# Issue steps of a prefetch and of two head copies in an attention and channel-mix kernel

## The chip, the cores and the metric

The kernel runs on one core of one Trainium2 chip. The metric is the device time of one execution in microseconds. The core has five engines that run side by side and wait for one another by semaphores: TensorE (PE, with its weight loads listed as PEld), VectorE (DVE), ScalarE (ACT), GpSimd (POOL) and SyncE (SP). SP computes nothing here; it issues DMA transfers, one after the other, in the order in which the program lists them.

## The reference, cut to what matters

Two layers follow each other. The first is attention through 32 inducing points, the second a channel mix with a gate.

```python
B, N, m, C = (4, 12608, 32, 128)      # d_ff = 1024
def mab(q, kv):
    s = scale * (q @ kv.transpose(0, 2, 1))
    s = s - s.max(-1, keepdims=True)
    a = np.exp(s)
    a /= a.sum(-1, keepdims=True) + 1e-09
    return a @ kv
h = mab(I, x)                         # 32 rows that sum up all tokens of a batch
x = mab(x, h)                         # each token attends to these 32 rows
...
xk = mu_k * x + (1.0 - mu_k) * x_prev # x_prev: the token before
xr = mu_r * x + (1.0 - mu_r) * x_prev
k = np.maximum(xk @ w_k, 0.0)
v = k * k @ w_v
r = 1.0 / (1.0 + np.exp(-(xr @ w_r)))
return (r * v).astype(np.float32)
```

## The kernel before

**Tiles and stages.** A batch of 12608 tokens is cut into 24 groups of 512 tokens and one of 320. Four groups make a block of 2048 tokens; a batch has six blocks and the tail. The kernel never forms the output of the first layer. It keeps the attention weights of the tokens towards the 32 rows (R, one tile for each group) and folds the 32 rows into the weights of the channel mix (W). The channel mix then reads R and W.

**The main loop.** It runs over 400 units, one to a step: four batches of 25 groups of 4 units, each unit a quarter of the 1024 hidden columns for one group. Step n does, in this order:

- `up` (L803): PE multiplies R with W into a PSUM tile ps_a of 2 x 512 columns (L809 and L811, four matmuls). There are two ps_a tiles.
- what was put down with `soon(n, ...)`; in the second step of a group then `zgate` (L790, PE at L798 and L799, ACT at L801).
- `square` (L815): VectorE makes k_t, the positive part, from ps_a (L821). Then kh, its square in a shorter format, comes from ACT (L826), or, for the steps in the set `high_vector`, from VectorE (L823). ACT squares k_t in place (L827), and GpSimd forms kl, the rest that kh leaves (L829).
- `store` of a finished pair of groups (VectorE L856, then four DMAs at L864).
- `down` (L832) for the unit of four steps earlier: PE multiplies kh and kl with the second weights (L840, six matmuls).
- what was put down with `at(n, ...)`.

So the order on every engine is written by hand: `at` puts work at the end of a step, `soon` puts it between `up` and the squares.

**The first layer beside it.** While batch b is in the main loop, the first layer of batch b+1 is worked off in blocks of 12 steps (`stage_a`, L326 to L483, first step t of a block). One load from HBM brings a block into xb, 1 MB (`load_x`, L193). There are three xb tiles. `btr(c)` (L339), in steps t-1, t, t+1 and t+3, turns a quarter of it on VectorE (L344) and spreads it with four DMAs of SP into xt (L347). In step t+9 PE makes the scores from xt (L372), VectorE takes their maximum (L375), and the rest of the softmax follows until step t+20. The second attention, for batch b itself, is `stage_b` (L598): its last part, `spread`, moves R into place in steps t+11 to t+14 with DMAs of SP (L593 and L670), which are steps t-1 to t+2 of the next block. All of these DMAs, and the output stores, stand in the one queue of SP.

The load of the next block is put down at the end of `stage_a` (L477 to L483), behind `btr(2)` of the same step:

```python
        for bn, jn in order_a[k + 1:]:
            if jn < NBLK - 1:
                at(t + 1, lambda: load_x(bn, jn))
```

With the second last block of a batch comes a small load of the tail (xl, L186).

**The head.** Before the first step, `head` works off the first layer of batch 0, and `start` (L995 to L1034) lays out the first groups of R. Groups 0 and 1 are made before step 0. Groups 2 and 3 are made in the first steps: ACT and VectorE make their parts in steps 3 and 4 (`high`, `low`), and `put` (L768) turns them with four transposes on PE (L771) into a PSUM tile and copies it to R on ACT (L773). `put` of group 2 is in step 6, that of group 3 in step 8. Group 2 is first read by `up` in step 8, group 3 in step 12.

```python
        for k, (high, low, put) in enumerate(pl1):
            at(3, high)
            at(4, low)
            at(2 * k + 6, put)
```

`high_vector` begins as `{3}` and receives two steps of each block of 12.

Of the kernel before, what the change touches and what calls it, by code (L numbers as in the profile page):

```python
# [19 lines left out]
def kernel(  # L20
# [138 lines left out]
    def groups(j):  # L159

        w = G if j < NBLK - 1 else TAIL // Q
        return [(j * BLK + i * w, w) for i in range(Q)]
# [16 lines left out]
    def load_x(b, j, pair=None, pieces=1):  # L179

        S = batches[b]
        gr = groups(j)
        w = gr[0][1]
        if w < G:
            t = xn_pool.tile([P, Q, C], F32, name="xl", bufs=1)
            nc.sync.dma_start(out=t[:w], in_=x[b, gr[0][0]:, :].rearrange("(i p) c -> p i c", p=w))  # L186
            for i in range(Q):
                S.xn[j, i] = t[:, i:i + 1, :]
            return
        src = x[b, j * BLK:(j + 1) * BLK, :].rearrange("(p s) c -> p s c", p=P)  # L190
        if b > 0:
            t = xn_pool.tile([P, Q * Q, C], F32, name="xb", bufs=3)
            nc.sync.dma_start(out=t, in_=src)  # L193
            S.xb[j] = t
            return
        if pair is not None:
            S.xh[j] = [next(pair).rearrange("p u (k c) -> p (u k) c", c=C) for _ in range(2)]
        else:
            t = xn_pool.tile([P, Q * Q, C], F32, name="xb", bufs=3)
            S.xh[j] = [t[:, :2 * Q, :], t[:, 2 * Q:, :]]  # L200
        n = 2 * Q // pieces
        for h in range(2):
            for o in range(0, 2 * Q, n):
                nc.sync.dma_start(out=S.xh[j][h][:, o:o + n, :], in_=src[:, 2 * Q * h + o:2 * Q * h + o + n, :])
# [121 lines left out]
    def stage_a(b, j, at, t):  # L326
# [8 lines left out]
        jt = NBLK - 1  # L335
# [141 lines left out]
        k = order_a.index((b, j))  # L477
        for bn, jn in order_a[k + 1:]:
            if jn < NBLK - 1:
                at(t + 1, lambda: load_x(bn, jn))  # L480
                if jn == NBLK - 2:
                    at(t + 1, lambda: load_x(bn, jt))
                break  # L483


# [102 lines left out]
    def halo(S, g, far=True):  # L588

        if g == 0:  # L590
            nc.vector.memset(S.R[g].bitcast(F32)[:, 0:1], 0.0)
        elif far:
            nc.sync.dma_start(out=S.R[g].bitcast(F32)[:, 0:1], in_=S.R[g - 1].bitcast(F32)[:, G:G + 1])  # L593
        else:
            nc.vector.tensor_copy(out=S.R[g][:, 0:1], in_=S.R[g - 1].bitcast(F32)[:, G:G + 1])
# [272 lines left out]
    def run(th):  # L868
        for f in th:
            f()  # L870
# [118 lines left out]
    def at(n, f):  # L989
        events.setdefault(n, []).append(f)  # L990

    def soon(n, f):
        early.setdefault(n, []).append(f)

    def start():  # L995

        part0, pl0 = stage_b_head([0, 1])
        part1, pl1 = stage_b_head([2, 3])
        sc0, tu0, df0, ex0, nm0 = part0([0])
        sc1, tu1, df1, ex1, nm1 = part0([1])  # L1000
        sc2, tu2, df2, ex2, nm2 = part1([0, 1])
        (hi0, lo0, put0), (hi1, lo1, put1) = pl0
        box = {}

        def bank():
            return pv.tile([P, G], F32, name="ps_v")

        def gate_bank(s):
            if s == 0:
                box["g"] = bank()  # L1010
            return box["g"][:, s * C:(s + 1) * C]

        wa = [wpart(s, 0, bank) for s in range(2)]
        wb = [wpart(s, 1, bank) for s in range(2)]
        wg = [wpart(s, None, lambda s=s: gate_bank(s)) for s in range(2)]
        assert F // G == 2
        S = batches[0]
        run([gates, sc0, sc1, tu0, df0, ex0, wa[0][0], wa[1][0], tu1, nm0, wa[0][1], hi0, wa[1][1], lo0, wa[0][2], put0,
             df1, ex1, wa[1][2], nm1, hi1, lambda: halo(S, 1, far=False)])
        for n, f in ((0, wb[0][0]), (0, wb[0][1]), (1, wb[1][0]), (1, wb[1][1]), (1, put1)):  # L1020
            soon(n, f)
        for n, f in ((0, lo1), (0, wb[0][2]), (1, wb[1][2]), (1, sc2), (2, tu2), (2, df2), (2, ex2), (3, nm2)):
            at(n, f)
        for prod, high, low in wg:
            at(1, prod)
        for prod, high, low in wg:
            at(1, high)
            at(2, low)
        for k, (high, low, put) in enumerate(pl1):
            at(3, high)  # L1030
            at(4, low)
            at(2 * k + 6, put)
            at(4 * k + 4, lambda k=k: halo(S, k + 2, far=False))
        soon(4, lambda: units[0][0].zgate(first=True))  # L1034

    SEG = 12
    high_vector = {3}
    for b in range(B):
        t = b * UB + (4 if b == 0 else 0)
        for j in range(NBLK - 1):  # L1040
            s = t + SEG * j
            high_vector |= {s + 4, s + 8}
            if b + 1 < B:
                stage_a(b + 1, j, at, s)
            first = b == 0 and j == 0
            stage_b(b, j + 1, at, s + 1 + first, first)
        if b + 1 < B:
            s = t + SEG * (NBLK - 1)
            combine(b + 1, at, s)
            stage_b(b + 1, 0, at, s + 13, b == 0)  # L1050
# [6 lines left out]
    with tc.manual_schedule():  # L1057
        head()
        start()
        for n in range(len(units) + LAG + 2):  # L1060
            grp, u = units[n] if n < len(units) else (None, n % NU)
            old, ou = units[n - LAG] if LAG <= n < len(units) + LAG else (None, 0)
            m = n - LAG - 1
            if 0 <= m < len(units) and units[m][1] == NU - 1:
                units[m][0].gate()
            if grp is not None:
                grp.up(u)
                run(early.pop(n, []))
                if n >= NU and u == 1:
                    grp.zgate()  # L1070
                low = grp.square(u, n in high_vector)
                low(nc.vector if n == end else nc.gpsimd, 0, grp.w)
            if 1 <= m <= len(units) and units[m - 1][1] == NU - 1:
                units[m - 1][0].store()
            if old is not None:
                old.down(ou)
            run(events.pop(n, []))
# [30 lines left out]
```

## Time and profile before

| what | value |
|---|---|
| time, median of 3 runs | 1131.95 us (1128.4 to 1132.33) |
| the profiled execution | 1130.93 us |
| its span, first to last instruction | 1128.7 us |
| granted TensorE clock, mean | 0.996 |
| squares kh on ACT and on VectorE | 351 and 49 |
| loads of x in the main loop's form (L193) | 18 |

The profiled execution is one run of its own; its time is longer than its span by what lies around the first and the last instruction. All rows below are of this one execution, and their times count from the start of its span.

A row of a timeline gives the start, the duration, the engine (SPq is the queue of SP), the line, the operation, out<-in, and, in brackets, how long the engine was idle before it and what ended that. Rows of one tile that follow each other are merged (x4). A row of waits gives who waited for whom, the total in us, how often, and the longest. A row of stretches gives the stretch, its length, the busy time of PE, PEld, DVE, ACT and POOL with the number of instructions, the granted clock, and the share and rate of DMA. Matmuls are pipelined, so a busy PE is not PE at its peak: a step of ten matmuls takes about 2.32 us, though each matmul is listed with 0.4.

### The profile page before, as it was taken

Reading aid. Unit: us, or ns where it says so; the run is one execution under the profiler, and the core shown is the slowest. Engines: PE = TensorE matmul, PEld = TensorE weight load, DVE = VectorE, ACT = ScalarE, POOL = GpSimd, SP = SyncE. Lnnn points to the kernel's source line nnn. Section 1 sums busy time; section 2 is a strip of 40 time slices with the busy share of each in tenths; the row PEclk is TensorE's granted clock in tenths of the full one; section 3 lists DMA queues with packets and bytes.
Section 4 is the critical chain, followed back from the end, with each engine's and each line's share of the span. In section 5 each row is a group of like instructions: output and inputs, shape, how many; then the busy total and the mean of one; then the engine's idle time right before and its main releaser. Section 6 shows DMA issues by size and latency. Waiting matters only on the chain.

```text
span 1128.7 us, 17615 instructions
## 1 busy us (share of the span) xinstructions
PE 1098.4 (97%) x5699; PEld 834.1 (74%) x5699; DVE 912.0 (81%) x1318; ACT 969.8 (86%) x1096; POOL 952.9 (84%) x417
## 2 busy tenths in 40 slices
PE   7889999999999999999999999999999999999997
PEld 5567777777776777777777777777778777777886
DVE  6798889887787999887777889898777888887665
ACT  6588888888888888887998889888889999989996
POOL 2279888888897888898888988888888899999997
PEclk9999999999999999999999999999999999999999
DMA  9024555642334655554144554654223233242212
GB/s 344 4 77 89 112 126 119 139 122 36 60 75 109 133 124 117 118 103 104 23 81 88 111 123 113 134 133 82 50 52 62 44 63 61 56 76 57 44 29 34
DMA packets 264458, 102.30 MB, mean 91 GB/s; under 512 B 234256, under 2 KB 237488, under 8 KB 262064
## 3 DMA queue, kind: packets, MB, share of 16 engines
q1 hardware_dynamic: 263360, 101.10, 41.0%
q8 instruction: 45, 0.74, 0.3%
q14 instruction: 45, 0.37, 0.1%
q10 hardware_dynamic: 1008, 0.10, 0.1%
HBM read 28.07 MB, written 25.82 MB: 48 GB/s over the span
## 4 chain that ended last, share of the span: by engine, by line
PE 78%; DVE 9%; ACT 5%; DMA 3%; issue 3%; SPq 1%; POOL 1%; DVEq 0%; ACTq 0%; POOLq 0%
PE ps_v L840 39%; PE ps_a L809 15%; PE ps_a L811 14%; DVE k_t L821 3%; PE pb_a L372 2%; PE pb_b L616 2%; ACT kh L826 2%; PE ps_v L798 2%; PE ps_v L799 2%; DMA xt<-xs 2%; PE pb_a L441 1%; ACT k_t L827 1%; SPq L347 1%; DMA xb<-in_x_dram 1%; POOL kl L829 1%
## 5 line engine op out<-in xcount | busy, mean ns | idle before, releaser
L829 POOL TENSOR_TENSOR kl<-k_t,kh 128x1024 fp32r<-128x1024 f32 (+1 forms) x399 | 938.5, 2385 | 140.7 <-ACT k_t L827 106.7
L821 DVE TENSOR_SCALAR k_t<-ps_a 128x1024 f32<-128x1024 f32 (+1 forms) x400 | 479.6, 1199 | 146.8 <-PE ps_a L811 123.2
L827 ACT ACTIVATE k_t<-k_t 128x1024 f32<-128x1024 f32 (+1 forms) x400 | 418.4, 1048 | 37.6 <-DVE kh L823 25.6
L826 ACT ACTIVATE kh<-k_t 128x1024 fp32r<-128x1024 f32 (+1 forms) x351 | 364.8, 1039 | 85.2 <-PE ps_v L840 49.5
L809 PE MATMUL ps_a<-R,W 128*128 128x512 f32 (+1 forms) x800 | 324.6, 406 | 4.1 <-ACT R L773 2.8
L811 PE MATMUL ps_a<-R,W 128*128 128x512 f32 (+1 forms) x800 | 314.6, 393 | 0.2 <-DVE W L543 0.2
L840 PE MATMUL ps_v<-kh,wvh 128*128 128x512 f32 (+1 forms) x800 | 247.8, 391 | 0.0
L840 PE MATMUL ps_v<-kl,wvh 128*128 128x512 f32 (+1 forms) x800 | 246.7, 390 | 0.7
L840 PE MATMUL ps_v<-kh,wvl 128*128 128x512 f32 (+1 forms) x800 | 247.0, 390 | 0.0
L809 PEld LDWEIGHTS ps_a<-R,W 128*128 128x128 f32 x800 | 151.2, 189 | 78.0 <-issue 14.4
L840 PEld LDWEIGHTS ps_v<-kl,wvh 128*128 128x128 f32 x800 | 148.5, 188 | 37.6 <-POOL kl L829 5.3
L840 PEld LDWEIGHTS ps_v<-kh,wvh 128*128 128x128 f32 x800 | 149.5, 188 | 34.7
L840 PEld LDWEIGHTS ps_v<-kh,wvl 128*128 128x128 f32 x800 | 149.5, 188 | 33.8
L811 PEld LDWEIGHTS ps_a<-R,W 128*128 128x128 f32 x800 | 150.9, 189 | 31.4 <-DVE W L543 0.8
L845 DVE TENSOR_TENSOR oT<-ps_v,rT 128x512 f32<-128x512 f32 (+1 forms) x100 | 66.6, 666 | 1.8
L856 DVE STREAM_TRANSPOSE ot<-oT 128x512 f32<-128x512 f32 x96 | 67.1, 699 | 0.0
L823 DVE SCALAR_TENSOR_TENSOR kh<-ps_a,k_t 128x1024 fp32r<-128x1024 f32 x49 | 60.0, 1224 | 5.1
L801 ACT ACTIVATE rT<-ps_v 128x512 f32<-128x512 f32 (+1 forms) x99 | 57.8, 584 | 0.3
L344 DVE STREAM_TRANSPOSE xs<-xb 128x512 f32<-128x512 f32 x72 | 49.9, 693 | 0.2
L801 ACT ACT_TABLE_LOAD x31 | 39.8, 1283 | 0.6
L798 PE MATMUL ps_v<-R,W 128*128 128x512 f32 (+1 forms) x99 | 39.0, 394 | 0.4 <-DVE oT L845 0.4
L799 PE MATMUL ps_v<-R,W 128*128 128x512 f32 (+1 forms) x99 | 38.7, 391 | 0.0
(211 smaller groups left out, 618.2 us busy)
## 6 DMA issues: line engine op xcount, KB each, us to landing
out_dram<-ot SPq DMA_DIRECT2D x184, 128.0 KB, 3.3
xb<-in_x_dram SPq DMA_DIRECT2D x18, 1024.0 KB, 6.1
xt<-xs SPq DMA_DIRECT2D x288, 64.0 KB, 2.0
R<-ah SPq DMA_DIRECT2D x184, 64.0 KB, 2.0
R<-al SPq DMA_DIRECT2D x184, 64.0 KB, 2.0
kl<-in_x_dram SPq DMA_DIRECT2D x4, 512.0 KB, 9.5
xb<-in_x_dram SPq DMA_DIRECT2D x4, 512.0 KB, 10.8
W<-ah SPq DMA_DIRECT2D x24, 64.0 KB, 2.0
```

What stands on the lines that cost most here:

```text
L798: nc.tensor.matmul(out=ps[:, :w], lhsT=S.W[0][:, F:WF], rhs=R[:, 1:w + 1], start=True, stop=False)
L799: nc.tensor.matmul(out=ps[:, :w], lhsT=S.W[1][:, F:WF], rhs=R[:, 0:w], start=False, stop=True)
L801: nc.scalar.activation(out=self.rT, in_=ps[:, :w], func=AF.Sigmoid)
L809: nc.tensor.matmul(out=ps[:, c, :w], lhsT=S.W[0][:, cs], rhs=R[:, 1:w + 1], start=True, stop=False)
L811: nc.tensor.matmul(out=ps[:, c, :w], lhsT=S.W[1][:, cs], rhs=R[:, 0:w], start=False, stop=True)
L821: nc.vector.tensor_scalar(out=k, in0=self.ps[:, :, :w], scalar1=0.0, scalar2=None, op0=ALU.max)
L826: nc.scalar.activation(out=kh, in_=k, func=AF.Square)
L827: nc.scalar.activation(out=k, in_=k, func=AF.Square)
L829: return lambda eng, a, z: eng.tensor_tensor(out=kl[:, :, a:z], in0=k[:, :, a:z], in1=kh.bitcast(F32)[:, :, a:z], op=ALU.subtract)
L840: nc.tensor.matmul(out=self.v, lhsT=wt[:, fc, :], rhs=kk[:, c, :], start=(fc == 0 and n == 0), stop=(fc == FC - 1 and n == 2))
L845: nc.vector.tensor_tensor(out=self.oT, in0=self.v, in1=self.rT, op=ALU.mult)
L856: nc.vector.transpose(out=ot[:, o:o + w], in_=self.oT)
```

## The change

Two places in the code, three effects. The load of the next block, and the tail's load, are put down four steps later. `put` of groups 2 and 3 stays in its step but goes from the end of the step to the place between `up` and the squares. The set `high_vector` begins empty instead of with step 3.

```diff
@@ stage_a
             if jn < NBLK - 1:
-                at(t + 1, lambda: load_x(bn, jn))
+                at(t + 5, lambda: load_x(bn, jn))
                 if jn == NBLK - 2:
-                    at(t + 1, lambda: load_x(bn, jt))
+                    at(t + 5, lambda: load_x(bn, jt))
                 break
@@ start
             at(3, high)
             at(4, low)
-            at(2 * k + 6, put)
+            soon(2 * k + 6, put)
             at(4 * k + 4, lambda k=k: halo(S, k + 2, far=False))
@@
-    high_vector = {3}
+    high_vector = set()
```

## The prediction

> **What bounds the kernel now.** I read the page's busy shares and its chain first.
>
> ```profile
> PE 1098.4 (97%) x5699; PEld 834.1 (74%) x5699; DVE 912.0 (81%) x1318; ACT 969.8 (86%) x1096; POOL 952.9 (84%) x417
> ```
>
> ```profile
> PE 78%; DVE 9%; ACT 5%; DMA 3%; issue 3%; SPq 1%; POOL 1%; DVEq 0%; ACTq 0%; POOLq 0%
> ```
>
> ```profile
> xb<-in_x_dram SPq DMA_DIRECT2D x18, 1024.0 KB, 6.1
> xt<-xs SPq DMA_DIRECT2D x288, 64.0 KB, 2.0
> ```
>
> TensorE (PE) is the engine to beat: it is busy 97% of the span and makes up 78% of the chain that ended last. No edit here removes matmuls, so the change can only win back time in which PE waits or runs slowly, and can only lose time by making PE wait elsewhere. DMA is 3% of the chain although it computes nothing: somewhere PE waits for data. The last two rows give the two transfers that matter: the 1 MB load of x into xb takes 6.1 us from issue to landing, a 64 KB piece of xt takes 2.0.
>
> Next I looked for the place. PE consumes xt in the score matmuls of L372, once in a block of 12 steps. I took the stretches from the first L809 matmul of such a step to the first of the next one; the columns are the stretch, its length, then busy times, granted clock and DMA. There are 18 such steps. The first row is an undisturbed one, and seven more are like it; the other ten are longer:
>
> ```profile
> 416.86:420.74 3.88, 3.88 (x22) 2.23 (x20) 3.45 (x5) 3.30 (x5) 3.88 (x2) 1.00 0.81 119
> 151.48:155.87 4.39, 4.39 (x22) 2.36 (x20) 3.63 (x5) 3.55 (x5) 4.39 (x3) 1.00 0.37 81
> 217.50:222.95 5.45, 4.74 (x21) 2.63 (x19) 3.48 (x5) 4.72 (x7) 5.45 (x3) 1.00 0.68 147
> 345.10:353.62 8.52, 5.81 (x21) 2.67 (x20) 4.36 (x5) 7.88 (x9) 8.45 (x4) 0.87 0.73 181
> 383.08:388.00 4.92, 4.92 (x22) 2.62 (x20) 3.29 (x5) 4.29 (x6) 4.92 (x3) 1.00 0.50 107
> 449.67:455.53 5.86, 4.86 (x21) 2.61 (x20) 3.35 (x5) 4.32 (x6) 5.86 (x3) 1.00 0.76 188
> 516.94:522.80 5.86, 4.81 (x22) 2.61 (x20) 3.35 (x5) 3.49 (x6) 5.69 (x3) 1.00 0.69 167
> 621.14:626.87 5.73, 4.85 (x21) 2.54 (x19) 4.39 (x5) 5.67 (x7) 5.63 (x3) 1.00 0.77 197
> 655.77:660.69 4.92, 4.33 (x22) 2.61 (x20) 3.30 (x5) 3.93 (x5) 4.92 (x3) 1.00 0.46 93
> 722.49:728.03 5.54, 4.75 (x22) 2.61 (x20) 3.43 (x5) 4.70 (x6) 5.54 (x3) 1.00 0.63 142
> 789.39:794.38 4.99, 4.99 (x21) 2.49 (x20) 3.36 (x5) 3.60 (x6) 4.99 (x3) 1.00 0.45 96
> ```
>
> Over 3.88 us each they lose, in this order, 0.51, 1.57, 4.64, 1.04, 1.98, 1.98, 1.85, 1.04, 1.66 and 1.11: 17.4 us, with the same matmuls in every one. That is the pool that the first edit fishes in.
>
> Why they are late is seen in the timeline of the SP queue, start and duration first. First come rows of the block behind the 449.67 row, then of the one behind the 345.10 row, the score matmuls of PE there, and a row of SP's waits (total, times, longest):
>
> ```profile
> 443.76 2.42 SPq L347 DMA_DIRECT2D xt<-xs  x4
> 446.27 0.53 SPq L193 DMA_DIRECT2D xb<-in_x_dram  x1
> 446.91 0.52 SPq L593 DMA_DIRECT2D R<-R  x1
> ```
>
> ```profile
> 450.07 2.96 SPq L347 DMA_DIRECT2D xt<-xs  x4
> ```
>
> ```profile
> 344.12 0.58 SPq L193 DMA_DIRECT2D xb<-in_x_dram  x1
> 344.79 2.41 SPq L347 DMA_DIRECT2D xt<-xs  x4
> ```
>
> ```profile
> 351.06 2.63 PE L372 MATMUL pb_a<-xt,indT 128*32 128x512 f32 x8 [2.69 <-DMA xb<-in_x_dram]
> ```
>
> ```profile
> SPq L347 <- DMA xb<-in_x_dram: 11.3, 13, 1.2
> ```
>
> SP issues in order and is behind: the last four xt pieces of the block leave at 450.07, in the very step that consumes them. The load stands ahead of them three times over. It takes an issue slot of 0.64 us (446.27 to 446.91). SP then waits for the load's landing before a later piece (11.3 us in 13 waits, 0.87 each). And pieces issued right behind it queue behind its 1 MB: those of 344.79 leave until 346.6 (three slots of 0.6 later) and would land by 348.6 with 2.0, yet PE starts at 351.06, when the load has landed.
>
> **The load, moved from step 1 to step 5.** At step 5 it stands behind the pieces of step 3. Nothing is added or removed: 18 loads stay 18, and the tail's xl load goes along. It is moved past the R pieces and the xt pieces of SP from 446.91 to 453, in some blocks past an output store as well, and past nothing on another queue. For an ordinary late block the last piece is issued 0.64 earlier (the slot) and its group takes 2.42 instead of 2.96, together 1.18: I take 1.2 off each of 1.98, 1.98 and 1.66, which is 3.6, and the full 0.51, 1.04, 1.04 from those that lose less than 1.2. The 217.50 block has the xl load out of the way too, a second slot of about 0.6, so I take its full 1.57. The 345.10 and 621.14 blocks have the pieces right behind the load; with 2.0 to land they are there before PE asks: 4.64 and 1.85. The 789.39 block has no load to move (it is the last of 18) and keeps its 1.11. Behind the long wait the clock is halved:
>
> ```profile
> 351.34:354.75 3.41, 3.41 (x11) 1.48 (x10) 0.69 (x1) 1.70 (x2) 3.41 (x3) 0.50 0.19 32
> ```
>
> Of these 3.41 us 1.13 lie behind 353.62, in the next step: half of that, 0.56, is lost there and comes back if the halving goes. Sum: 3.6 + 2.59 + 1.57 + 4.64 + 1.85 + 0.56 = 14.8 us.
>
> That the halving goes with the wait is my reading of one place. [...]
>
> What is late next? The load itself. It must land before VectorE copies from xb at the next block's step -1. Three kinds of block:
>
> ```profile
> 460.92 0.71 DVE L344 STREAM_TRANSPOSE xs<-xb 128x512 f32<-128x512 f32 x1
> ```
>
> ```profile
> 411.95 3.25 SPq L347 DMA_DIRECT2D xt<-xs  x4
> 415.43 2.94 SPq L864 DMA_DIRECT2D out_dram<-ot  x4
> ```
>
> ```profile
> 426.48 0.71 DVE L344 STREAM_TRANSPOSE xs<-xb 128x512 f32<-128x512 f32 x1
> ```
>
> ```profile
> 347.30 3.67 SPq L864 DMA_DIRECT2D out_dram<-aT  x4
> ```
>
> ```profile
> 359.63 0.71 DVE L344 STREAM_TRANSPOSE xs<-xb 128x512 f32<-128x512 f32 x1
> ```
>
> ```profile
> DMA to landing us min/median/max: 5.5/6.2/11.8
> ```
>
> Store behind the load: pieces end at 450.07 - 0.64 + 2.42 = 451.9, the load lands 6.1 later at 458.0, VectorE asks at 460.92 - 1.2 = 459.7: 1.7 us to spare. Store ahead of it (step 5 itself): pieces end at 413.7, the store takes 2.94, the load lands at 422.8, VectorE asks at 426.48: 3.7 to spare. First block of a batch, with the aT store ahead: pieces end at 346.5, the store takes 2.4 to 3.67 (four slots of 0.6, or as now), the load lands at 355.1 to 356.3, VectorE asks at 359.63 - 5.2 = 354.4: 0.7 to 1.9 short, at two places. VectorE is ahead of PE (below), so I bound this between 0 and 2 x 1.9 and take **0.5**. What queues behind the load are the output store and the next block's R pieces, which PE reads a block later: nothing. SP's total work is unchanged.
>
> **The copies of groups 2 and 3, and the square of step 3.** The set that sends squares to VectorE loses its 3, so the square kh of unit 3 goes to ScalarE (ACT). This square does move, from one engine to another.
>
> ```profile
> 60.42 1.22 DVE L823 SCALAR_TENSOR_TENSOR kh<-ps_a,k_t 128x1024 fp32r<-128x1024 f32 x1
> ```
>
> ```profile
> 61.67 1.06 ACT L827 ACTIVATE k_t<-k_t 128x1024 f32<-128x1024 f32 x1 [1.86 <-DVE kh L823]
> ```
>
> ```profile
> 61.79 0.47 PE L809 MATMUL ps_a<-R,W 128*128 128x512 f32 x1 [0.66 <-DVE kh L823]
> ```
>
> ```profile
> 72.58 0.57 ACT L773 CAST R<-pb_a 128x512 fp32r<-128x512 f32 x1
> ```
>
> ```profile
> 73.21 0.49 PE L809 MATMUL ps_a<-R,W 128*128 128x512 f32 x1 [2.09 <-ACT R L773]
> ```
>
> ACT is idle for 1.86 us before 61.67, waiting for that very kh. It can make it itself from 60.42 on: with two squares of 1.06 it is done with both at 62.5 to 62.6, where it is done at 62.73 now, and VectorE is 1.22 us ahead. PE's 0.66 at 61.79 goes, since no square on VectorE reads ps_a any more. R's copy of group 2 stands at 72.58 behind the two squares of its step; in front of them it ends 2 x 1.06 = 2.1 us earlier, and PE's wait of 2.09 in front of step 8 goes. New waits: the four transposes that feed the copy now need their PSUM bank from ACT's gate of the step before, at about the time when PE comes to them (bounds 0 and 1.06, one pass of ACT as above; I take 0, because ACT loses its 1.86 of idling just before). The squares behind the copies come 0.57 later and are used four steps on. Sum: 0.66 + 2.09 = **2.7 us**.
>
> Total: 14.8 + 2.7 - 0.5 = 17.0. The profiled execution took 1130.93 (span 1128.7 and 2.2 around it), giving 1113.9; it lies 1.0 below the median of the runs, so against 1131.95 I forecast **1115**.
>
> **Rivals.** *The load comes too late and VectorE stops (slower).* Of 18 loads, three are for a first block and one falls where SP is still idle; fourteen have a near deadline. Two rows on the cushions:
>
> ```profile
> DVE k_t L821 <- PE ps_a L811: 123.2, 141, 2.4
> PEld ps_v L840 <- POOL kl L829: 5.3, 14, 0.6
> ```
>
> VectorE waits for PE 141 times, 0.87 us each: that much delay costs nothing. With margins of 1.7 to 3.7 (middle 2.7) the turning point is a landing of 6.1 + 2.7 + 0.9 = 9.7 us. At the longest landing seen, 11.8, it costs 14 x 2.1 = 29 us: 1115 + 29 = **1144**. For it: the load now shares the queues with an output store. Against it: of the loads inside the loop the median is 6.1. [...] Chance 0.07.
>
> *SP is late by itself.* The 789.39 step loses 1.11 without any load ahead. If backlog rather than the load is the cause in the ordinary late blocks, only the two blocks whose pieces stand right behind a load gain: 4.64 + 1.85 + 0.56 + 2.7 = 9.8, **1122**. The same figure comes if the start gives nothing and half of the ordinary blocks stay late. Chance 0.21.
>
> *Another wait takes the place.* POOL's kl ends PE's waits 14 times already (5.3 us), at 84% busy. If PE, once ahead, meets kl or ACT's squares in the steps behind, the gain is given back: about **1130**. Against it: POOL's idle time is 16% of the span. Chance 0.11.
>
> **How the numbers follow.** Forecast (1110 to 1118.5): 0.59; better than 1110, by something outside the sum: 0.02; rivals 0.21, 0.11, 0.07. The range 1110 to 1126 leaves out 0.20. A difference of 0.5% (5.7 us) is about what a measurement can tell: faster 0.82, same 0.11, slower 0.07.
>
> **What would show it.** Right: the ten steps at 3.88 but for three near 4.6 and the last at 5.0; no halved clock behind 350; no PE wait for R near 73; the load's issue behind the xt pieces; 48 squares on VectorE. Wrong: L344 waiting for xb by more than 1 us, PE waiting for kl in the steps behind the scores, or the xt pieces no earlier.

## The result, and the profile after

| | before | after |
|---|---|---|
| time, median (lowest to highest) | 1131.49 us (1127.04 to 1132.41, 6 runs) | 1118.66 us (1115.97 to 1120.37, 6 runs) |
| the profiled execution (its span) | 1130.93 us (1128.7) | 1118.96 us (1116.7) |
| squares kh on ACT and on VectorE | 351 and 49 | 352 and 48 |

The ratio is 0.9895, with a 95% interval from 0.9873 to 0.9917. The change makes the kernel about 1% faster: 12.8 us by the medians and 12.0 by the profiled executions, where 17.0 were forecast. The time lies inside the range of 1110 to 1126, but as near to the 1122 of the rival *SP is late by itself* as to the forecast of 1115; the time alone doesn't choose between them.

First the page of the changed kernel: the busy shares, the chain, the group of VectorE's copies out of xb, and the load of x.

```profile
PE 1094.6 (98%) x5699; PEld 831.1 (74%) x5699; DVE 910.9 (82%) x1317; ACT 969.8 (87%) x1097; POOL 952.8 (85%) x417
...
PE 85%; DVE 7%; ACT 3%; issue 2%; DMA 1%; POOL 1%; SPq 1%; DVEq 0%; POOLq 0%; ACTq 0%
...
L344 DVE STREAM_TRANSPOSE xs<-xb 128x512 f32<-128x512 f32 x72 | 49.9, 694 | 4.3 <-DMA xb<-in_x_dram 3.8
...
xb<-in_x_dram SPq DMA_DIRECT2D x18, 1024.0 KB, 5.7
```

DMA falls from 3% of the chain to 1%, and PE's share grows from 78% to 85%. The third row is new: VectorE has to wait 3.8 us for the load.

Next the steps with scores, in the view of stretches that the prediction used (stretch, length, busy times of PE, PEld, DVE, ACT and POOL, clock, DMA). Two rows are other steps: 346.59 is the one behind the score step of 342.01, and 485.20 is an early step of the next block.

```profile
150.23:154.37 4.14, 4.14 (x22) 2.36 (x20) 3.35 (x5) 3.84 (x6) 4.14 (x2) 1.00 0.58 127
215.99:219.87 3.88, 3.88 (x22) 2.24 (x20) 3.77 (x5) 3.01 (x6) 3.88 (x2) 1.00 0.63 145
342.01:346.59 4.58, 4.58 (x22) 2.29 (x20) 4.34 (x5) 4.51 (x5) 4.53 (x2) 1.00 0.50 98
346.59:348.99 2.40, 2.40 (x11) 1.99 (x11) 1.79 (x2) 2.37 (x5) 2.40 (x2) 1.00 0.73 154
375.53:379.41 3.88, 3.88 (x22) 2.23 (x20) 3.30 (x5) 3.29 (x5) 3.88 (x2) 1.00 0.61 166
441.08:445.31 4.23, 4.23 (x21) 2.36 (x19) 3.36 (x5) 3.67 (x5) 4.23 (x3) 1.00 0.61 124
485.20:490.25 5.05, 3.43 (x21) 2.14 (x19) 3.68 (x5) 1.53 (x3) 2.76 (x2) 1.00 0.28 61
508.67:514.21 5.54, 5.47 (x22) 2.63 (x20) 3.35 (x5) 4.29 (x6) 5.54 (x3) 1.00 0.55 115
612.89:617.11 4.22, 4.13 (x21) 2.15 (x19) 4.11 (x5) 4.16 (x5) 4.12 (x2) 1.00 0.57 93
645.96:650.37 4.41, 4.41 (x21) 2.37 (x20) 3.58 (x5) 3.94 (x6) 4.41 (x2) 1.00 0.50 112
712.17:716.16 3.99, 3.99 (x21) 2.34 (x19) 3.44 (x5) 3.42 (x5) 3.99 (x2) 1.00 0.55 126
777.62:782.40 4.78, 4.78 (x22) 2.50 (x20) 3.36 (x5) 3.77 (x6) 4.78 (x3) 1.00 0.38 83
```

The ten late steps are those of the prediction, in the same order; their excess over 3.88 us falls from 17.4 to 4.9 us (0.26, 0, 0.70, 0, 0.35, 1.66, 0.34, 0.53, 0.11, 0.90). The step of 8.52 us is now 4.58. The granted clock is 1.00 in every stretch, and the step at 346.59 takes 2.40 us. In before that step still had the end of the halving in it, with a clock of 0.81 and 2.92 us (second row):

```profile
495.45:498.63 3.18, 3.18 (x22) 2.23 (x20) 3.18 (x5) 2.41 (x3) 3.06 (x2) 1.00 0.36 83
353.62:356.54 2.92, 2.92 (x12) 2.40 (x12) 1.79 (x2) 0.00 (x0) 2.92 (x2) 0.81 0.00 0
```

The first row is the step that became the 485.20 one: 3.18 us before, 5.05 after. There the change loses 1.87. The queue of SP and VectorE of the changed kernel show why (start, duration, engine, line, tile; in brackets the idle time ahead and what ended it):

```profile
471.04 3.23 SPq L347 DMA_DIRECT2D xt<-xs  x4
474.37 3.04 SPq L864 DMA_DIRECT2D out_dram<-ot  x4
477.51 0.68 SPq L193 DMA_DIRECT2D xb<-in_x_dram  x1
478.23 0.76 SPq L186 DMA_DIRECT2D xl<-in_x_dram  x1
```

```profile
486.57 0.71 DVE L344 STREAM_TRANSPOSE xs<-xb 128x512 f32<-128x512 f32 x1 [2.68 <-DMA xb<-in_x_dram]
```

The load now stands behind the xt pieces, as it should, but behind an output store too. It leaves at 477.51 and lands at 486.55, 9.0 us later. VectorE had come for it at 483.89.

Put together, from the first `up` matmul of each step in the two profiled executions: the 18 score steps give 12.5 us, the step behind the halving 0.5, the head (step 0 to step 12) 1.8; the step at 485.20 takes 1.87 back, and some 1.0 us is lost in small pieces, 0.47 of them before step 0, where no edit reaches. That sums to 12.0.

### The profile page after: what moved, and what is told of

The parts are those of the page before. It is cut to its first block, busy times and chain, and to the rows that moved or that the text cites. A ratio compares the mean times of both kernels' runs of the same rounds, so it can differ in the third digit from the quotient of the medians.

```text
span 1116.7 us, 17642 instructions
## 1 busy us (share of the span) xinstructions
PE 1094.6 (98%) x5699; PEld 831.1 (74%) x5699; DVE 910.9 (82%) x1317; ACT 969.8 (87%) x1097; POOL 952.8 (85%) x417
## 4 chain that ended last, share of the span: by engine, by line
PE 85%; DVE 7%; ACT 3%; issue 2%; DMA 1%; POOL 1%; SPq 1%; DVEq 0%; POOLq 0%; ACTq 0%
PE ps_v L840 43%; PE ps_a L809 16%; PE ps_a L811 15%; DVE k_t L821 2%; PE pb_b L616 2%; PE pb_a L372 2%; PE ps_v L798 2%; PE ps_v L799 2%; PE pb_a L441 2%; ACT kh L826 1%; DMA xb<-in_x_dram 1%; POOL kl L829 1%; ACT k_t L827 1%; PE ps_a L227 1%; DVE oT L845 1%
## 5 line engine op out<-in xcount | busy, mean ns | idle before, releaser
L344 DVE STREAM_TRANSPOSE xs<-xb 128x512 f32<-128x512 f32 x72 | 49.9, 694 | 4.3 <-DMA xb<-in_x_dram 3.8
```

## The experiments

All times are medians, compared with runs of the kernel before on the same chip. "Excess" is what the 18 score steps of the profiled execution take over 3.88 us each; it is 17.3 before and 4.8 after (eight steps at 3.86 to 3.88 count slightly below zero). Where the pieces are late, the excess differs from execution to execution: e2_head, e5_put and e6_hv have the loop of before, and their profiled executions have 14.1, 19.6 and 16.9. "Head" is the time from the first `up` matmul of step 0, or 3, to that of step 12.

### The parts alone

**e1_load5.** The load at step 5, nothing else.

```diff
-                at(t + 1, lambda: load_x(bn, jn))
+                at(t + 5, lambda: load_x(bn, jn))
```

> Only the load is moved (step 5); the head's copies and the square of step 3 stay as before. Theory (the load in front of the xt pieces made the score steps late): between the profiles of before and after, the steps from unit 37 on account for 10.7 us of the 12.0, so this kernel takes about 1131.5 - 11 = 1120.5, the score steps are as short as in the changed kernel, and PE still waits some 2 us for R in front of step 8. Rival (the head gives most of it and the loop's steps follow): under 4 us faster, 1128 or more.

Measured: 1119.72 us, ratio 0.9905 (0.9886 to 0.9925). Excess 4.9; VectorE waits for xb three times, 4.3 us in all.

**e2_head.** The changed kernel with the load back at step 1, so the two edits of the head alone.

```diff
-                at(t + 5, lambda: load_x(bn, jn))
+                at(t + 1, lambda: load_x(bn, jn))
```

> Only the head is changed (copies in front of the squares, no square of step 3 on VectorE); the load stays in step 1. Theory: PE's waits of 2.09 and 0.66 us go, VectorE takes back about 1 us in steps 9 to 11, so 1.3 to 1.8 us faster: about 1130, and all ten late score steps are late as before. Rival (the head gives most): 8 us or more faster. Second rival (VectorE and ACT take back all): the same as before.

Measured: 1129.17 us, ratio 0.9982 (0.9969 to 0.9994). Head from step 0: 34.38 us, where before takes 36.02. The profiled execution is the fastest of the ten (1126.07). By the medians the load brings 11.6 us and the head 2.1.

### Where the load should stand

**e3_load3.** The changed kernel with the load at step 3. There it is still behind the last xt pieces of its block, but ahead of a store that falls in step 5.

```diff
-                at(t + 5, lambda: load_x(bn, jn))
+                at(t + 3, lambda: load_x(bn, jn))
```

> The changed kernel with the load in step 3 instead of 5: still behind the last xt pieces, but ahead of the output store of step 5. Theory (the load lands late, 7 to 9 us, because it stands behind a store, and VectorE then waits for it): the loads of those blocks land in 5.3 to 6.5 us, VectorE's wait for xb (3.8 us in the changed kernel) falls below 0.8, the step of 5.05 us near 495 of before is 3.2 again and the score step behind it shrinks by about 1: 1118.7 - 2.8 = 1116. Rival (the late landing is chance, whatever the order): 1118.7, with a wait for xb of 2 us or more somewhere.

Measured: 1114.33 us, ratio 0.986 (0.9844 to 0.9877), faster than both kernels. The step that lost 1.87 us is back at 3.18, the one after it stays late. First the two steps in the view of stretches, then SP and VectorE of the same place:

```profile
483.37:486.55 3.18, 3.18 (x22) 2.23 (x20) 3.18 (x5) 2.42 (x4) 2.84 (x3) 1.00 0.46 104
504.86:510.45 5.59, 5.49 (x21) 2.62 (x19) 3.35 (x5) 3.92 (x6) 5.59 (x3) 1.00 0.53 119
```

```profile
473.20 0.53 SPq L193 DMA_DIRECT2D xb<-in_x_dram  x1
...
474.32 6.16 SPq L864 DMA_DIRECT2D out_dram<-ot  x4
```

```profile
481.72 0.71 DVE L344 STREAM_TRANSPOSE xs<-xb 128x512 f32<-128x512 f32 x1
```

The load leaves at 473.20, ahead of the store, and is there 5.9 us later; VectorE waits for nothing. Of the loads in the changed kernel, the seven that stand right behind the store of a pair of groups (out_dram<-ot, four times 128 KB) take 6.4 to 9.0 us to land (6.4, 6.9, 7.1, 6.7, 9.0, 7.4, 7.2). The ten others inside the loop take 5.2 to 5.9, among them the two behind the small last store of a batch (out_dram<-aT, four times 40 KB) with 5.4 and 5.5. At step 3 none stands right behind a store, and the seventeen take 5.2 to 6.5. So the store ahead of the load is what made it late, by its place in the queue and by the longer landing.

**e4_load10.** The changed kernel with the load at step 10, to see the price of the first rival.

```diff
-                at(t + 5, lambda: load_x(bn, jn))
+                at(t + 10, lambda: load_x(bn, jn))
```

> The changed kernel with the load in step 10: behind every output store, one step ahead of the step that copies it. Theory (the load has a deadline, VectorE's first copy, and a small cushion): in the seven or so blocks whose store is in step 9 the load is issued some 4 us later and VectorE waits 2 to 4 us in each; the xt pieces of the next block follow late; 10 to 20 us slower than the changed kernel, 1129 to 1139. Rival (VectorE's lead over PE covers it): within 2 us of the changed kernel.

Measured: 1159.45 us, ratio 1.0246 (1.0207 to 1.0286). The direction is that of the theory, the price larger. VectorE's waits, with total, number and longest:

```profile
DVE xs L344 <- DMA xb<-in_x_dram: 34.3, 6, 8.3
```

A seventh wait of 4.6 us is put down to another DMA that ended beside it. The profiled execution is the fastest of the four (1151.25 at a mean granted clock of 0.988, the others 1159.3 to 1162.2 at 0.977 to 0.979). VectorE's 39 us in it come close to the 37.2 that lie between it and the profiled execution with step 3 (1114.07); PE stops with VectorE, and six of the seven times its granted clock is 0.50 behind the wait, the seventh time 1.00. With steps 3, 5 and 10 at 1114.3, 1118.7 and 1159.5 us, the change as made stands already on the slope.

### What the load costs at step 1

**e7_actq.** The kernel before, with the load at step 1 issued by ACT.

```diff
-            nc.sync.dma_start(out=t, in_=src)
+            nc.scalar.dma_start(out=t, in_=src)
```

> The kernel before, with x's load still at step 1 of a block but issued on ACT's queue, so that it leaves SP's queue and its bytes alone stay in the way. Theory (the xt pieces of a score step are late because they stand in SP's queue behind the issue of the 1024 KB load): the pieces reach the queue earlier by the load's share of SP's time, the score steps come down towards the 3.88 us of the plain ones, excess over 3.88 about 5 to 8 us in the 18 of them where before had 17.3, time about 1120. Rival (the load's bytes share the 16 DMA engines with the pieces, whichever queue issues them): the pieces land as late as before, excess about 17, time about 1131.

Measured: 1181.19 us, ratio 1.0447 (1.0418 to 1.0476); both were wrong. The load lands sooner (4.7 to 6.3 us), yet excess is 64 us. The waits and the queue of SP in this kernel:

```profile
SPq L670 <- DMA xb<-in_x_dram: 84.5, 12, 7.7
```

```profile
132.06 0.53 SPq L593 DMA_DIRECT2D R<-R  x1
140.30 0.51 SPq L670 DMA_DIRECT2D R<-ah  x1
```

ACT issues this load at 134.91, it lands at 140.28, and SP, which has issued only one of the DMAs that the program lists behind the load, stands still for 7.7 us until then. Why an R piece has to wait for a load on another queue is seen in the operands of the DMA instructions in the trace. All 1145 DMAs of the program, on SP and ACT together, report their landing on one of eight semaphores, used in turn, and in the traces of before and of the changed kernel none leaves before the DMA that had its semaphore before it has landed (the closest leaves 0.02 us behind it). The load of 134.91 and the R piece of 140.30 both have semaphore 102; why the turn falls on these two is not shown. So the run doesn't part the slot from the bytes; it shows that SP's waiting for a landing is worth more than either. SP's 13 waits of before have the same reason: each ends 0.02 us behind the landing of the load eight places ahead in the queue.

**e9_split.** The kernel before, with the load of step 1 as two DMAs of 512 KB.

```diff
-            nc.sync.dma_start(out=t, in_=src)
+            nc.sync.dma_start(out=t[:, :2 * Q, :], in_=src[:, :2 * Q, :])
+            nc.sync.dma_start(out=t[:, 2 * Q:, :], in_=src[:, 2 * Q:, :])
```

> The kernel before, with the load of step 1 split into two DMAs of 512 KB: the same bytes at the same step, but one more issue in SP's queue ahead of the xt pieces. Theory (the slot in SP's queue is what costs): each late score step grows by about one more issue, some 0.3 to 0.6 us, in 16 steps +5 to +9 us, time about 1136 to 1140. Rival (the bytes cost): no change, 1131.

Measured: 1135.16 us, ratio 1.0035 (1.0013 to 1.0058). That is 4.6 us by the medians (1130.54 for before), with the same bytes. In the profiled execution, the slowest of the ten (1140.17), the excess is 23.7, and SP's wait for the load's landing grows from 11.3 us to 14.6 (one line number further down in this kernel):

```profile
SPq L348 <- DMA xb<-in_x_dram: 14.6, 11, 2.7
```

So one more issue ahead of the pieces costs something, a little less than was expected of the slot. How much of it is the slot and how much SP's longer wait is not shown: the excess is 6.4 above that of before, but only 4.1 above that of e5_put, which has the loop of before.

### Is it the load at all?

**e8_store.** The version with the load at step 3, and the store that falls in step 1 of a block put behind the last xt pieces as well.

```diff
+                if n in late:
+                    at(n + 3, put)
+                else:
+                    put()
...
+                late.add(s + 1)
```

> The version with the load at step 3 (1114.3 us), with the output store of the unit that ends in step 1 of a block moved behind the last xt piece as well. Theory (what is left in the score steps, 3.5 us over 3.88 in all, is SP's queue late by the store in front of the pieces): the steps at 109, 145, 169, 209, 221 and 269 come down to about 3.9, time 1111 to 1112. Rival (the rest is not the queue: a late piece of x, or transposes that are late by themselves): the steps stay, 1114.3.

Measured: 1111.78 us, ratio 0.9837 (0.981 to 0.9864). Excess 0.6. The steps that were late in the changed kernel at 342.01, 441.08, 508.67 and 777.62 are here:

```profile
341.56:345.75 4.19, 4.19 (x22) 2.16 (x20) 4.08 (x5) 4.13 (x5) 4.14 (x2) 1.00 0.92 275
440.24:444.13 3.89, 3.89 (x22) 2.23 (x20) 3.36 (x5) 3.33 (x5) 3.89 (x2) 1.00 0.96 282
...
505.53:509.40 3.87, 3.87 (x21) 2.23 (x19) 3.35 (x5) 2.54 (x5) 3.87 (x3) 1.00 0.87 263
771.80:775.70 3.90, 3.90 (x21) 2.23 (x19) 3.36 (x5) 2.54 (x5) 3.90 (x3) 1.00 0.72 111
```

Three of the four are plain steps now, the first keeps 0.31 (and the step that was at 612.89 keeps its 0.35). What the load's move left in the score steps was the store in front of the pieces.

**e11_store1.** The same, with the load back at step 1: only the store moved, beside the head's edits.

```diff
-                at(t + 3, lambda: load_x(bn, jn))
+                at(t + 1, lambda: load_x(bn, jn))
```

> The version with the store behind the last xt piece (1111.8 us), with the load back at step 1, in front of the pieces of step 3. Theory (the load in front of the pieces costs by itself: its slot, and SP's wait for its landing): the excess of the 18 score steps over 3.88 goes from 0.6 to about 8 to 12 us, time 1119 to 1123. Rival (the load cost only because the stores had already made SP late): the excess stays below 3 us, time 1112 to 1114.

Measured: 1112.14 us, ratio 0.9839 (0.9811 to 0.9867). Excess 0.8. The rival is right: the load stands in front of the pieces as it did before the change, and costs nothing. Three views of this kernel: its SP queue at the place that the prediction showed at 450.07, SP's waits, and the score step there.

```profile
431.34 0.52 SPq L193 DMA_DIRECT2D xb<-in_x_dram  x1
431.97 0.52 SPq L593 DMA_DIRECT2D R<-R  x1
...
435.13 3.36 SPq L347 DMA_DIRECT2D xt<-xs  x4
438.53 7.42 SPq L865 DMA_DIRECT2D out_dram<-ot  x8
```

```profile
SPq L347 <- DMA xb<-in_x_dram: 11.2, 13, 1.9
```

```profile
439.18:443.06 3.88, 3.88 (x21) 2.23 (x19) 3.35 (x5) 3.33 (x5) 3.88 (x2) 1.00 0.86 137
```

SP still waits 11.2 us for the load to land, 13 times, as before (11.3, 13). But the last pieces leave at 435.13, 4.0 us ahead of the step that uses them (439.18); before they left 0.4 us into it (450.07 against 449.67). A delay of about a microsecond in front of work that is 4 us early is not seen. So the load at step 1 was not the cause by itself. Load and store together made the pieces late, and taking either out of their way is enough for most blocks. With the head's edits in all four, the medians are (the runs of before beside them have 1130.5 to 1131.3):

| | store where it was | store behind the pieces |
|---|---|---|
| load at step 1 | 1129.17 us (e2_head) | 1112.14 us (e11_store1) |
| load at step 3 | 1114.33 us (e3_load3) | 1111.78 us (e8_store) |

Moving the load alone gains 14.8 us, the store alone 17.0, both 17.4.

### The head

**e5_put** and **e6_hv.** The two edits of the head one by one, on the kernel before, one execution each: R's copies in front of the squares, and the square of step 3 on ACT.

```diff
-            at(2 * k + 6, put)
+            soon(2 * k + 6, put)
```

> The kernel before, with only R's copies of groups 2 and 3 in front of the step's squares; the copy of k of group 3 stays on VectorE and the load at step 1. Theory (the wait of 2.09 us for R at step 8 is the order of ScalarE's queue): that wait goes, the 0.66 us at step 5 stays; head from step 0 to step 12 about 34.5 to 35 us where before had 36.0, time about 1129 to 1130. Rival (R's copies wait for their own input and not behind the squares): the wait stays at about 2, time 1131.

```diff
-    high_vector = {3}
+    high_vector = set()
```

> The kernel before, with only the square of step 3 moved from VectorE to ScalarE; R's copies stay behind the squares and the load stays at step 1. Theory (the wait of 0.66 us at step 5 is PE waiting for VectorE's long square, and ScalarE's idle 1.86 us takes the square): step 4 gets shorter by about 0.8 us, and the wait of about 2 us for R in front of step 8 stays; from step 3 to step 12 about 26.7 us where before had 27.55. Rival (ScalarE is full and passes the square on): step 4 shortens, but step 7 grows by the same, 27.5 us.

Measured: 1132.07 and 1131.14 us, which a single execution can't tell from before. In the profiles both waits go as expected. For the gain I count from step 3, since the steps 0 to 2, which no edit touches, differ by up to 0.8 us between these executions: 27.54 us before, 26.92 with the copies, 26.49 with the square, 25.86 with both. So the copies are worth 0.62 and the square 1.05. The same stretches of step 7, and of steps 8 to 11, in before and in the changed kernel:

```profile
68.57:73.21 4.64, 2.55 (x14) 1.78 (x12) 3.49 (x6) 4.58 (x7) 4.52 (x3) 1.00 0.59 132
73.21:83.44 10.23, 10.23 (x46) 8.38 (x47) 9.16 (x14) 10.09 (x12) 7.73 (x4) 1.00 0.30 100
```

```profile
68.42:70.81 2.39, 2.39 (x14) 1.99 (x11) 1.09 (x1) 2.36 (x4) 2.27 (x2) 1.00 0.38 87
70.81:82.13 11.32, 10.62 (x48) 8.06 (x46) 10.89 (x17) 11.17 (x13) 9.02 (x5) 1.00 0.38 116
```

Step 7 loses its 2.25 us. The four steps behind it give 1.09 back: there ACT is busy for 11.17 of 11.32 us and VectorE for 10.89, and PE, which never stopped there before (10.23 of 10.23), now waits for them for 0.70.

**e10_kh8.** The fastest version (e8_store) with one more square, that of step 8, moved from VectorE to ACT.

```diff
-            high_vector |= {s + 4, s + 8}
+            high_vector |= {s + 4, s + 8} - {8}
```

> The version with the load at step 3 and the store behind the last xt piece (1111.8 us), with one more square, that of step 8, moved from VectorE to ScalarE. Theory (from step 7 on VectorE alone holds the head up: PE waits for its k_t at 77 and 82 us): those waits of 0.23 and 0.47 us go, steps 9 and 11 fall from 3.17 and 2.96 us towards 2.4, time lower by 0.7 to 1.2, about 1110.8. Rival (ScalarE is busy without a break there as well): the time moves over to ScalarE's squares, 1111.8 or up to 1 us more.

Measured: 1113.71 us, ratio 0.9853 (0.9821 to 0.9885). That is 1.9 us above e8_store, with intervals of the ratio that overlap; the rival had allowed 1. From step 3 to step 12 it takes 25.78 us, where e8_store takes 25.85. Step 9 falls from 3.17 to 2.77, and step 12 grows from 2.37 to 3.27. The rival is right in kind: ACT has no room for the square either; where the other microsecond comes from is not shown. Both engines bound these steps.

## Why the prediction was right, and where its sizes were off

The direction and the range held, and so did the chain of the forecast: the xt pieces leave earlier, PE waits less in the score steps, and the halved clock goes with the long wait. The reason given for the lateness was half of it: the load costs because the stores have already made SP late. A sign named for being wrong came true as well, L344 waiting for xb by more than 1 us (3.8). Of the forecast 17.0 us 12.0 came, with every term short on the same side, and each can be put beside its measurement.

**The load's move: 14.8 forecast, 13.0 measured** (12.5 in the score steps, 0.5 in the step behind the halving; by the medians the load alone brought 11.6). That pieces queue behind the 1 MB was read rightly: in before the four right behind the load of 344.12 took 5.1 to 6.2 us to land, where the usual is 2.0. The step from "one issue slot and the shorter group" to the full recovery of the small blocks was too generous. I took the full 0.51 and 1.04 of some blocks, and 4.64 and 1.85 of two others; they kept 0.26, 0.53, 0.70 and 0.34. The block of 508.67 kept 1.66, where I left it 0.78; two others kept 0.35 and 0.11 of my 0.78 and 0.46. That these last three sum up to 3.5 us, where I had 3.6, is luck: they gained 0.32, 1.63 and 1.55, and not 1.2 each. I named the load as what stands in front of the pieces "three times over" and did not look further up the queue, where the store stands. In the block of 450.07 it is this row of before:

```profile
436.70 3.01 SPq L864 DMA_DIRECT2D out_dram<-ot  x4
```

The order of the program could have told it without a run. Of the 18 blocks, eight have such a store in their step 1, and these are the eight late ones besides those of 345.10 and 621.14, that of 789.39 without a load among them; none of the eight plain ones has it. e8_store and e11_store1 show it: with the store behind the pieces the excess is 0.6 or 0.8, wherever the load is. The rival *SP is late by itself* had this cause right, though not its size, since taking out the load alone was enough for most blocks.

**The head: 2.7 forecast, 1.7 measured** from step 3 on, and divided the other way. The wait of 2.09 in front of step 8 went as forecast, but the copies brought 0.62. "The squares behind the copies come 0.57 later and are used four steps on" was the failing sentence: it asked when the squares are needed, and not whether ACT and VectorE have time left once PE stops less. The row of before had the answer, with ACT at 10.09 of 10.23 us. The square brought 1.05, more than PE's visible wait of 0.66: step 4 shrinks by 0.82, steps 5 to 7 by 0.26 together.

**The cost of the late load: 0.5 forecast, 1.87 measured** in the one step that grew most; a second wait of 1.08 us cost little. I looked for it in the first blocks of a batch, which came out 0.7 to 1.9 short in my sum; they never waited. It came in the class for which I had 3.7 us to spare. Two things were wrong there. I took 9.8 us between the load's issue and VectorE's coming (426.48 less the end of the store at 416.6), by moving SP's rows of one block forward and leaving VectorE's where they were. In the changed kernel that very block has 7.1 (410.43 and 417.53): its pieces and its store leave later against VectorE than the sum had it. Of the seven blocks behind such a store five have 6.1 to 7.7 (that of 477.51 has 6.4), one has 11.4, and one has no near deadline. And I took 6.1 us to land for every load, while the seven behind a store took 6.4 to 9.0. The rival *The load comes too late* was thus true at two loads and costly at one, and three more of that class had less than 1 us to spare; e4_load10 shows what it costs where it is true in seven. The first blocks of a batch had 0.3 and 1.8 us to spare.

**Right as forecast:** the clock (0.51 us came back in the step behind, 0.56 forecast; that half the clock follows a wait of 2.69 us doesn't hold for every longer one, see the last section), no PE wait for R near 73, 48 squares on VectorE, and POOL's kl, which ends 6.0 us of PE's weight loads' waits where it ended 5.3. The rival *Another wait takes the place* happened in the head, by ACT and VectorE.

## What to carry to other kernels

When a transfer is late in an in-order queue, list everything that stands between its producer and it, and ask what is the longest of it that nobody needs soon; here the output store of 3 us was as good a choice as the 1 MB load that the wait pointed at (17.0 us against 14.8). Move a prefetch behind the urgent pieces but no further: each place beyond that is paid out of its own deadline, and a margin that is worked out by moving rows of one queue needs a reserve, since the other engines move too (9.8 us became 7.1 here). When a queue waits for the landing of a transfer that it doesn't need, look whether the two share a semaphore. A wait that goes from one engine is worth only what the engines behind it have idle in the next few steps, not over the span (in the head here 1.7 us came of the forecast 2.7).

## What the runs showed of the hardware

**Loads right behind a large store took longer to land.** In the changed kernel the same 1 MB takes 5.2 to 5.9 us to land behind xt pieces or a store of four times 40 KB, and 6.4 to 9.0 behind a store of four times 128 KB (6.2 to 8.9 in e1_load5). It is no clean line: at step 1, behind xt pieces as well, the loads of before take 5.5 to 7.5.

**A load on another engine's queue was no way out.** In e7_actq SP waited 84.5 us for loads that ACT had issued. By the medians the kernel lost 50.7 us (1181.19 against 1130.54). SP stood still until the other queue's load had landed, by the eight semaphores that this program's DMAs share; a load with a semaphore of its own was not tried.

**The length of PE's wait alone did not tell whether the clock was halved.** Three waits of PE, the first of e2_head, the others of e4_load10, each with the clock behind it:

```profile
350.03 1.47 PE L372 MATMUL pb_a<-xt,indT 128*32 128x512 f32 x6 [2.52 <-DMA xb<-in_x_dram]
```

```profile
407.02 0.64 PE L798 MATMUL ps_v<-R,W 128*128 128x512 f32 x1 [2.84 <-DVE oT L845]
```

```profile
756.73 0.50 PE L798 MATMUL ps_v<-R,W 128*128 128x512 f32 x1 [3.26 <-DVE oT L845]
```

```profile
350.38:352.03 1.65, 1.65 (x9) 0.59 (x8) 0.07 (x1) 1.62 (x2) 1.65 (x2) 1.00 0.37 60
```

```profile
408.02:409.02 1.00, 1.00 (x4) 0.80 (x3) 1.00 (x3) 0.83 (x1) 0.00 (x0) 0.50 0.43 98
757.08:760.33 3.25, 3.25 (x18) 1.76 (x17) 3.25 (x5) 2.39 (x3) 0.14 (x1) 1.00 0.38 81
```

After 2.52 us of waiting the clock is 1.00, after 2.84 it is 0.50 (as after the 2.69 of before), and after 3.26 it is 1.00 again. What it hangs on besides is not shown. That the halving goes with the wait was read from one place. It came true in the changed kernel, where the clock is 1.00 from 51.93 to 1113.40 us, but these rows show that it need not have.
